# Padded loads of decays, keys and receptances, and an opening with five plain slices, in a recurrence with a gated MLP behind it

## The chip, the cores and the metric

The program runs on one core of one Trainium2 chip. The metric is device time in microseconds, from an execution without the profiler. The kernel before was executed three times for it: 574.48, 574.70 and 574.89 us, a median of 574.7 us. All durations below come from one further execution that the hardware profiler recorded.

## The reference

Four sequences, 8 heads of 48 channels and 768 steps go through a recurrence with a decay per channel; its output is the input of a gated MLP with 3072 rows, model width 384 and inner width 1536.

```python
for t in range(S):                       # r, k, v, w: [4, 8, 768, 48]
    cur = einsum('bhd,bhe->bhde', u[None] * kt, vt)
    y[:, :, t] = einsum('bhd,bhde->bhe', rt, state + cur)
    state = wt[:, :, :, None] * state + einsum('bhd,bhe->bhde', kt, vt)
x = y.transpose(0, 2, 1, 3).reshape(B * S, H * D)
gate = 1 / (1 + exp(-(x @ w_gate)))
out = (gate * (x @ w_val)) @ w_out
```

## The kernel before, in words

**Tiling.** The 768 steps are cut into six chunks of 128. A *unit* q is one chunk of one sequence; there are 24, and four units with consecutive q (one per sequence, the same chunk) make a round of 512 rows. For each unit the kernel loads two tiles. `pin` holds decays, keys and receptances with channels on 112 partitions, 1544 numbers in a row; `tok` holds receptances, keys and values with time on 128 partitions, 1152 numbers in a row. The attention of a unit is: running products of the decays on VectorE (`prep_k`, `prep_r`), a transposition of the keys (`turn_k`, tile `pk`), scores and sums on TensorE (`section1`, tile `pa`), a mask and the new state on VectorE (`mask`, `keep`), the output products (`section2`, tile `py`), a copy by ScalarE (`take_y`), a transposition (`turn_x`, tile `px`), and a copy that makes the MLP's input (`take_x`). GpSimd prepares the diagonal (`bonus1`, `bonus2`, `bonus4`, tiles `bon` and `at`).

**The MLP.** The inner width is cut into 12 slices f of 128. The weights of a slice come as words of 64 bits (`raw`) that VectorE turns into numbers of 32 bits in three steps (`w_body`, `w_sign`, `w_tail`), while ScalarE checks their range with two passes (`w_guard`, tile `sq`). A slice is then used in one of two ways. A *plain* slice is multiplied as float32 (lines 527 and 569). A *split* slice first gets a high and a low part (`w_hi`, `w_lo`), and so does x, and three products of float32r stand for one (lines 530, 533 and 573). For each slice there are a gate product (`pg`), a value product (`pu`), a sigmoid, VectorE's product of the two, and an output product (`po`). There is one bank for `pg` and one for `pu`.

**The order.** The rounds 1 to 5 have an order written out by hand, the same in every round. Round 0, the preparation of the weights, and the first units of round 1 together are the *opening*. Its order comes from a planner (class `Plan`) at build time: each operation has an engine, a cost, a rank and conditions, and a list scheduler emits the operations in the order in which its own clock starts them. `TURNS` gives the ranks, `COMES` the order in which loads are issued on SyncE's queue, `LATE` and `LAGS` shift ranks, `ROOM` counts buffers. On the chip each engine then runs its instructions strictly in that order, waiting where data is not there.

Before the change the slices 0 to 3 are plain in round 0, each in two groups of units, (0, 1) and (2, 3), 256 columns at a time; the slices 4 to 11 are split, with all 512 columns. Behind the scores of units 0 and 1 stand 11 and 12 products of the identity with itself (`busy`, line 451), whose result nothing reads.

Of the kernel before, what the change touches and what calls it, by code (L numbers as in the profile page):

```python
# [205 lines left out]
def tile_kernel(ctx: ExitStack, tc: tile.TileContext, dec: bass.AP, tok: bass.AP, wts: bass.AP, u: bass.AP, out: bass.AP):  # L206
# [86 lines left out]
    def place(q):  # L293
        return q % B * NC_ + q // B

    def load_pin(q):
        t = p2.tile([L, WW + 2 * NP * C], F32, tag="pin", name=f"pin{q}")
        if q == 0:
            nc.sync.dma_start(t[:, :WW], dec[place(q)][:, :WW])
            nc.sync.dma_start(t[:, WW:], dec[place(q)][:, WW:])  # L300
        else:
            nc.sync.dma_start(t, dec[place(q)])
        pin[q] = t
# [526 lines left out]
```

## Time and profile before

| | us |
|---|---|
| median of three runs | 574.7 |
| the profiled execution, its own time | 575.17 |
| its span from first to last instruction | 573.1 |
| TensorE busy | 548.7 (96%) |
| VectorE busy | 325.0 (57%) |
| ScalarE busy | 204.3 (36%) |
| GpSimd busy | 104.2 (18%) |
| start of the first MLP product (round 0) | 31.41 |
| start of the first MLP product of round 1 | 139.29 |

The profiled execution lies 0.47 us above the median, and 2.1 us of it lie outside the span. A row of the timeline gives the start and length of a run of like instructions on one engine, then line, operation, output and inputs, and in brackets how long the engine was idle before it and what ended that. TensorE's float32 instructions appear twice for each product in the program, so x6 stands for three products. Successive products overlap, so the pace of a run is read from the distance between starts, not from the length of one. VectorE and ScalarE instructions overlap by about 0.1 us in the same way.

### The profile page before, as it was taken

How to read it: one execution, taken by the hardware profiler on the slowest of the kernel's cores; microseconds unless marked ns; L12 is line 12 of the kernel's file. 1: busy time of each engine (PE TensorE's matmuls, PEld its weight loads, DVE VectorE, ACT ScalarE, POOL GpSimd, SP SyncE). 2: the span in 40 equal slices, each digit the busy share in tenths (PEclk: the TensorE clock that was granted, in tenths of full speed). 3: DMA queues.
4: the chain of work that ended last, by engine and by line, in shares of the span. 5: the costliest groups of instructions: out<-in, count | busy, mean ns of one | idle time of the engine just before them, and what ended most of it. 6: DMA issues, size and time to landing. Idle time of an engine off the chain costs nothing.

```text
span 573.1 us, 13259 instructions
## 1 busy us (share of the span) xinstructions
PE 548.7 (96%) x5910; PEld 452.3 (79%) x5910; DVE 325.0 (57%) x451; ACT 204.3 (36%) x376; POOL 104.2 (18%) x89
## 2 busy tenths in 40 slices
PE   5789999999999999999999999999999999999994
PEld 4667877888778888888888888878888888888883
DVE  4899999997774564653563653653643621321221
ACT  2565775734442322422223323222413322312111
POOL 4440634104022111221210220210220200000000
PEclk9799999999999999999999999999999999999999
DMA  8856927424213023123033133032122000100001
GB/s 251 267 173 249 312 78 270 117 66 147 73 46 91 21 72 91 63 85 91 1 92 91 56 91 91 2 91 92 55 92 65 27 2 2 55 2 0 1 0 61
DMA packets 11044, 50.57 MB, mean 88 GB/s; under 512 B 1265, under 2 KB 1266, under 8 KB 9442
## 3 DMA queue, kind: packets, MB, share of 16 engines
q1 hardware_dynamic: 8818, 45.70, 25.7%
q10 hardware_dynamic: 2160, 3.93, 1.8%
q8 instruction: 48, 0.79, 0.6%
q14 instruction: 18, 0.15, 0.1%
HBM read 44.91 MB, written 4.72 MB: 87 GB/s over the span
## 4 chain that ended last, share of the span: by engine, by line
PE 83%; DVE 9%; issue 2%; ACT 2%; DMA 1%; POOL 1%; SPq 0%; ACTq 0%; DVEq 0%; POOLq 0%
PE po L573 23%; PE pg L530 16%; PE pu L530 15%; PE pu L533 8%; PE pg L533 8%; PE py L432 3%; PE py L419 3%; PE pa L403 1%; PE pa L390 1%; PE pk L371 1%; DMA tok<-tok 1%; DVE temp L273 1%; PE px L486 1%; DVE raw L276 1%; PE busy L451 1%
## 5 line engine op out<-in xcount | busy, mean ns | idle before, releaser
L550 DVE TENSOR_TENSOR sg<-pu,sg 128x512 f32<-128x512 f32 (+1 forms) x76 | 50.3, 662 | 160.9 <-PE pu L533 155.8
L573 PE MATMUL po<-hh,w 128*128 128x512 f32 x408 | 129.6, 399 | 0.0
L530 PE MATMUL pg<-x,w 128*128 128x512 f32 x408 | 106.7, 397 | 0.0
L530 PE MATMUL pu<-x,w 128*128 128x512 f32 x408 | 104.3, 391 | 0.0
L530 PEld LDWEIGHTS pu<-x,w 128*128 128x128 f32 x408 | 76.3, 188 | 15.9
L530 PEld LDWEIGHTS pg<-x,w 128*128 128x128 f32 x408 | 75.0, 188 | 16.5
L573 PEld LDWEIGHTS po<-hh,w 128*128 128x128 f32 x408 | 74.2, 188 | 13.8
L543 ACT ACTIVATE sg<-pg 128x512 f32<-128x512 f32 (+1 forms) x76 | 43.4, 571 | 113.3 <-PE pg L533 109.7
L554 ACT CAST hh<-sg 128x512 fp32r<-128x512 f32 x68 | 42.2, 620 | 116.5 <-DVE sg L550 116.4
L573 PE MATMUL po<-hl,w 128*128 128x512 f32 x204 | 79.8, 391 | 0.1
L558 DVE TENSOR_TENSOR hl<-sg,hh 128x512 fp32r<-128x512 f32 x68 | 51.9, 763 | 42.3 <-ACT hh L554 42.2
L320 POOL TENSOR_TENSOR bon<-tok,ub 128x384 f32<-128x384 f32 x24 | 29.2, 1215 | 230.5 <-DMA tok<-tok 199.2
L533 PE MATMUL pg<-x,w 128*128 128x512 f32 x204 | 57.6, 391 | 0.0
L533 PE MATMUL pu<-x,w 128*128 128x512 f32 x204 | 57.6, 391 | 0.0
L333 POOL TENSOR_TENSOR at<-eye,a 128x512 f32<-128x512 f32 x24 | 32.4, 1351 | 119.2 <-DVE a L327 119.2
L573 PEld LDWEIGHTS po<-hl,w 128*128 128x128 f32 x204 | 38.4, 188 | 9.2 <-DVE hl L558 0.7
L533 PEld LDWEIGHTS pg<-x,w 128*128 128x128 f32 x204 | 38.3, 188 | 8.2
L533 PEld LDWEIGHTS pu<-x,w 128*128 128x128 f32 x204 | 38.3, 188 | 8.0
L323 POOL TENSOR_TENSOR bon<-bon,tok 128x384 f32<-128x384 f32 x24 | 39.6, 1650 | 1.9
L340 DVE TENSOR_TENSOR_SCAN eg<-pin,ends 112x516 f32<-112x516 f32 x24 | 35.9, 1495 | 7.0 <-DMA pin<-dec 7.0
L366 ACT ACTIVATE eg<-eg 112x1032 f32<-112x1032 f32 x24 | 25.6, 1068 | 36.6 <-DVE pin L362 35.4
L481 ACT COPY bon<-py 128x384 f32<-128x384 f32 x24 | 11.5, 478 | 61.3 <-PE py L432 61.3
(80 smaller groups left out, 654.2 us busy)
## 6 DMA issues: line engine op xcount, KB each, us to landing
pin<-dec SPq DMA_DIRECT2D x23, 675.5 KB, 6.2
tok<-tok SPq DMA_DIRECT2D x24, 576.0 KB, 6.1
raw<-wts SPq DMA_DIRECT2D x12, 1152.0 KB, 12.2
y<-o ACTq DMA_DIRECT2D x15, 256.0 KB, 2.0
y<-o SPq DMA_DIRECT2D x3, 256.0 KB, 3.4
pin<-dec SPq DMA_DIRECT2D x1, 448.0 KB, 4.8
pin<-dec SPq DMA_DIRECT2D x1, 227.5 KB, 3.6
line<-u SPq DMA_DIRECT2D x1, 1.5 KB
```

Source lines behind the costliest of these rows:

```text
L320: nc.gpsimd.tensor_tensor(out=bon[q], in0=tk[q][:, 0:DM], in1=ub, op=ALU.mult)
L323: nc.gpsimd.tensor_tensor(out=bon[q], in0=bon[q], in1=tk[q][:, DM:2 * DM], op=ALU.mult)
L333: nc.gpsimd.tensor_tensor(out=att[q], in0=eye.unsqueeze(1).unsqueeze(1).broadcast_to(shape), in1=a0, op=ALU.mult)
L340: nc.vector.tensor_tensor_scan(out=e[:, 516:0:-1], data0=t[:, 516:0:-1], data1=ends[:, 516:0:-1], initial=0.0, op0=ALU.mult, op1=ALU.add,)
L366: nc.scalar.activation(both, both, AF.Square, accum_out=acc_d[:, q:q + 1])
L530: nc.tensor.matmul(t, lhsT=w[f][:, cols], rhs=x[n][:, a, k, spot], start=k == 0 and j == 0, stop=False)
L533: nc.tensor.matmul(t, lhsT=whi[f][:, cols], rhs=x[n][:, 1, k, i0 * C:i1 * C], start=False, stop=k == NKT - 1)
L543: nc.scalar.activation(sg, hid["g", n, f, i0], AF.Sigmoid)
L550: nc.vector.tensor_tensor(out=sg, in0=hid["u", n, f, i0], in1=sg, op=ALU.mult)
L554: nc.scalar.copy(hh, hid["s", n, f, i0])
L558: nc.vector.tensor_tensor(out=hl, in0=hid["s", n, f, i0], in1=hid["hi", n, f, i0].bitcast(F32), op=ALU.subtract)
L573: nc.tensor.matmul(to, lhsT=w[f][:, cols], rhs=h, start=first and i == 0, stop=last and i == 2, skip_group_check=True)
```

## The change

**Loads.** The array `dec` on the host gets 128 rows of 1664 numbers for each unit instead of 112 rows of 1544. The keys begin at number 528 instead of 520. A load of `pin` moves 128 rows of 1552 numbers (unit 0 in two parts, 528 and 1024), and the rows 112 to 127 are not used.

**The opening.** Five slices are plain, 0 to 4, and seven are split. The plain slices 0, 1 and 4 are cut into three groups, unit 0 alone, unit 1 alone and units 2 and 3, so that 128 columns are multiplied at a time for the first two; 2 and 3 keep two groups. The planner's ranks and several of its costs are new. The products of the identity are 40 members of the planner's list with the lowest rank, instead of two runs at fixed places; they and the spreading of u use the banks of `po` until the MLP needs these.

```diff
-TURNS = "c0 w0 w1 c1 w2 c2 w3 c3 c4 c5 w4 w5 w6 w7 w8 w9 w10 c6 w11 c7"
-COMES = "p0 ub t0 p1 t1 w0 w1 w2 p2 t2 t3 p3 w3 p4 w4 t4 w5 w6 t5 p5 w7 t6 w8 t7 w9 w10 w11 p6 p7 p8 t8 t9 p9"
-GROUPS = [(0, 2), (2, 4)]
-WIDE = [4, 5, 6, 7, 8, 9, 10, 11]
-EXACT = [0, 1, 2, 3]
+TURNS = "c0 w0 w1 c1 w2 c2 w3 c3 c4 w4 w5 c5 w6 w7 w8 w9 w10 w11 c6 c7"
+COMES = "p0 ub w0 t0 w1 p1 w2 w3 t1 w4 t2 p2 t3 w5 p3 w6 t4 t5 p4 p5 t6 w7 w8 w9 w10 w11 p6 p7 t7 t8 p8 p9 t9"
+SINGLE = [0, 1, 4]
+WIDE = [5, 6, 7, 8, 9, 10, 11]
+EXACT = [0, 1, 2, 3, 4]
...
-        t = p2.tile([L, WW + 2 * NP * C], F32, tag="pin", name=f"pin{q}")
...
+        t = p2.tile([P, KW + 2 * NP * C], F32, tag="pin", name=f"pin{q}")
+        for i, j in ((0, KW), (KW, KW + 2 * NP * C)) if q == 0 else ((0, KW + 2 * NP * C),):
+            nc.sync.dma_start(t[:, i:j], dec[place(q)][:, i:j])
+        pin[q] = t[:L]
...
-        if q in BUSY:
-            t = ps1.tile([P, 512], F32, tag="po0", name=f"busy{q}")
-            for _ in range(BUSY[q]):
-                nc.tensor.matmul(t[:, :P], lhsT=ident, rhs=ident, start=True, stop=True)
...
+    def keep_busy():
+        nc.tensor.matmul(lull[:, :P], lhsT=ident, rhs=ident, start=True, stop=True)
+
+    lull = ps1.tile([P, 512], F32, tag="po0", name="lull")
+    for i in range(BUSY):
+        add(f"busy{i}", "PE", 0.43 if i < 9 else 0.28, [i and f"busy{i - 1}"], 1000 + i, keep_busy)
...
+    parts = {f: ([(0, 1), (1, 2), (2, B)] if f in SINGLE else [(0, 2), (2, B)]) if f in EXACT else [(0, B)] for f in range(NFF)}
...
-    dec = np.zeros((NG, L, WW + 2 * NP * C), np.float32)
+    dec = np.zeros((NG, P, ROW), np.float32)
```

**What moves, on SyncE's queue.** The first loads that SyncE issues before the change; `pin` and `tok` belong to the units 0, 0, 1, 1, 2 and 2 in turn, `raw` to the slices 0, 1 and 2:

```order
L299 DMA pin_106<-dec 112x520
L300 DMA pin_106<-dec 112x1024
L611 DMA line<-u 1x384
L307 DMA tok_110<-tok 128x1152
L302 DMA pin_118<-dec 112x1544
L307 DMA tok_130<-tok 128x1152
L258 DMA raw_181<-wts 128x1152
L258 DMA raw_248<-wts 128x1152
L258 DMA raw_314<-wts 128x1152
L302 DMA pin_368<-dec 112x1544
L307 DMA tok_381<-tok 128x1152
```

The same place in the changed kernel, with `raw` of the slices 0 to 4 and `tok` of the units 0, 1 and 2:

```order
L301 DMA pin_107<-dec 128x528
L301 DMA pin_107<-dec 128x1024
L603 DMA line<-u 1x384
L260 DMA raw_116<-wts 128x1152
L306 DMA tok_129<-tok 128x1152
L260 DMA raw_141<-wts 128x1152
L301 DMA pin_191<-dec 128x1552
L260 DMA raw_205<-wts 128x1152
L260 DMA raw_228<-wts 128x1152
L306 DMA tok_287<-tok 128x1152
L260 DMA raw_293<-wts 128x1152
L306 DMA tok_342<-tok 128x1152
```

The weights of slice 0 now stand ahead of `tok` of unit 0, and four slices ahead of `tok` of unit 1.

**On TensorE.** The first MLP products before the change, with what stands just ahead of them (`py` and `px` are of unit 1; `pg_0_0` is slice 0 of the group that begins with unit 0):

```order
L451 MATMUL busy_291<-ident 128x128 x12
L419 MATMUL py_327<-mid_318,pin_118 64x48 x8
L432 MATMUL py_327<-tok_130,at_306 32x48 x32
L486 MATMUL px_374<-ident,bon_193 128x128 x3
L527 MATMUL pg_0_0_387<-whole,raw_181 128x256 x3
L527 MATMUL pu_0_0_392<-whole,raw_181 128x256 x3
L527 MATMUL pg_0_1_405<-whole,raw_248 128x256 x3
L371 MATMUL pk_415<-ident,pin_368 128x112 x4
L569 MATMUL po_0_423<-sg_0_0_402,raw_181 128x256
L569 MATMUL po_1_424<-sg_0_0_402,raw_181 128x256
```

And in the changed kernel, from the first MLP product on:

```order
L519 MATMUL pg_0_0_349<-whole,raw_116 128x128 x3
L519 MATMUL pu_0_0_356<-whole,raw_116 128x128 x3
L519 MATMUL pg_0_1_367<-whole,raw_141 128x128 x3
L561 MATMUL po_0_374<-sg_0_0_360,raw_116 128x128
L561 MATMUL po_1_375<-sg_0_0_360,raw_116 128x128
L561 MATMUL po_2_376<-sg_0_0_360,raw_116 128x128
L519 MATMUL pu_0_1_383<-whole,raw_141 128x128 x3
L561 MATMUL po_0_374<-sg_0_1_388,raw_141 128x128
L561 MATMUL po_1_375<-sg_0_1_388,raw_141 128x128
L561 MATMUL po_2_376<-sg_0_1_388,raw_141 128x128
L418 MATMUL py_404<-mid_347,pin_191 64x48 x8
L431 MATMUL py_404<-tok_287,at_381 32x48 x32
```

The slices 0 and 1 of unit 0 are now multiplied ahead of the output products of unit 1 (`py_404`), which stood ahead of the first MLP product before.

**On ScalarE.** Around the first sigmoid before the change (`sq` are the range checks of slices 1 and 2):

```order
L265 ACTIVATE sq_322,acc_s<-raw_248 128x1152
L266 ACTIVATE sq_322,acc_t<-sq_322 128x1152
L481 COPY bon_193<-py_327 128x2x4x48
L514 CAST x_372<-whole 128x3x128
L509 ACTIVATE whole,acc_x<-px_374 128x3x128
L265 ACTIVATE sq_384,acc_s<-raw_314 128x1152
L266 ACTIVATE sq_384,acc_t<-sq_384 128x1152
L543 ACT_TABLE_LOAD
L543 ACTIVATE sg_0_0_402<-pg_0_0_387 128x256
L514 CAST x_372<-whole 128x3x128
L543 ACTIVATE sg_0_1_420<-pg_0_1_405 128x256
```

And in the changed kernel (`sq` of slices 3 and 4; `whole` is unit 0, `bon_305` is unit 1):

```order
L501 ACTIVATE whole,acc_x<-px_301 128x3x128
L467 COPY mid_347<-pa_307 112x192
L506 CAST x_353<-whole 128x3x128
L535 ACT_TABLE_LOAD
L535 ACTIVATE sg_0_0_360<-pg_0_0_349 128x128
L267 ACTIVATE sq_364,acc_s<-raw_228 128x1152
L268 ACTIVATE sq_364,acc_t<-sq_364 128x1152
L535 ACTIVATE sg_0_1_388<-pg_0_1_367 128x128
L267 ACTIVATE sq_390,acc_s<-raw_293 128x1152
L268 ACTIVATE sq_390,acc_t<-sq_390 128x1152
L476 COPY bon_305<-py_404 128x2x4x48
```

The range checks of slices 3 and 4 now stand between the first sigmoids and ahead of the copy of unit 1's output; three checks stood ahead of the first sigmoid before.

## Rows read from the trace of the kernel before

**Rows 1.** The page's first part: busy time of each engine, its share of the span and its instructions.

```profile
PE 548.7 (96%) x5910; PEld 452.3 (79%) x5910; DVE 325.0 (57%) x451; ACT 204.3 (36%) x376; POOL 104.2 (18%) x89
```

**Rows 2.** Busy time of each engine (TensorE's products and weight loads, VectorE, ScalarE, GpSimd) in a stretch of the span (in us), with the granted clock, the busy share of the 16 DMA engines and what they moved in GB/s.

```profile
200.00:300.00 100.00, 100.00 (x1053) 82.54 (x1052) 53.56 (x78) 29.39 (x58) 18.36 (x14) 1.00 0.24 72
```

**Rows 3.** TensorE's timeline in the opening.

```profile
5.07 1.61 PE L609 MATMUL spread<-line 1*128 1x384 f32 x2 [5.07 <-DMA line<-u]
...
8.72 1.13 PE L390 MATMUL pa<-pin 48*64 48x64 f32 x32 [0.46 <-DVE pin L362]
...
17.97 0.55 PE L486 MATMUL px<-ident,bon 128*128 128x128 f32 x3 [0.60 <-ACT bon L481]
...
21.98 0.88 PE L403 MATMUL pa<-tok,kT 64*64 64x48 f32 x23 [2.69 <-issue]
22.79 5.34 PE L451 MATMUL busy<-ident 128*128 128x128 f32 x24
28.06 0.67 PE L419 MATMUL py<-mid,pin 48*64 48x48 f32 x16
28.66 0.88 PE L432 MATMUL py<-tok,at 64*32 64x48 f32 x64
...
31.41 1.57 PE L527 MATMUL pg<-whole,raw 128*128 128x256 f32 x6 [0.67 <-ACT whole L509]
...
38.77 1.46 PE L527 MATMUL pu<-whole,raw 128*128 128x256 f32 x6
40.06 1.46 PE L527 MATMUL pg<-whole,raw 128*128 128x256 f32 x6
...
99.16 1.53 PE L530 MATMUL pg<-x,w 128*128 128x512 f32 x6
...
105.29 1.52 PE L530 MATMUL pg<-x,w 128*128 128x512 f32 x6
...
139.29 1.53 PE L530 MATMUL pg<-x,w 128*128 128x512 f32 x6
```

**Rows 4.** Whom TensorE waited for from its first MLP product to the first of round 1 (31.4 to 139.29 us): total in us, times, longest.

```profile
PE pg L527 <- ACT sg L543: 1.4, 1, 1.4
PE po L569 <- DVE sg L550: 0.9, 3, 0.4
PE pg L527 <- ACT whole L509: 0.7, 1, 0.7
PE pk L371 <- ACT whole L509: 0.7, 1, 0.7
PE py L419 <- DVE state L478: 0.5, 1, 0.5
```

**Rows 5.** The same columns as Rows 2, for three stretches chosen by what the queue carried in them: weights of slices 0 to 2; `pin` and `tok` of unit 2; `pin` of units 6 and 7 alone.

```profile
12.00:20.00 8.00, 6.33 (x146) 5.62 (x145) 7.90 (x11) 2.69 (x7) 6.51 (x4) 1.00 1.01 428
20.00:26.00 6.00, 4.02 (x38) 3.93 (x38) 4.46 (x6) 4.69 (x8) 0.26 (x1) 0.58 0.94 223
102.00:107.00 5.00, 5.00 (x24) 4.14 (x23) 4.96 (x6) 3.85 (x6) 0.55 (x1) 1.00 0.90 227
```

**Rows 6.** VectorE's timeline in the opening.

```profile
4.57 1.23 DVE L340 TENSOR_TENSOR_SCAN eg<-pin,ends 112x516 f32<-112x516 f32 x1 [4.57 <-DMA pin<-dec]
...
7.97 0.69 DVE L362 TENSOR_TENSOR pin<-pin,eg 112x512 f32<-112x512 f32 x1
11.69 0.55 DVE L327 TENSOR_REDUCE a<-bon 128x8 f32<-128x384 f32 x1 [3.02 <-POOL bon L323]
...
14.78 0.72 DVE L463 COPY_PREDICATED at<-after,pa 128x512 f32<-128x512 int32 x1
15.41 0.34 DVE L478 TENSOR_TENSOR state<-pa,mid 112x192 f32<-112x192 f32 x1
...
16.91 1.31 DVE L362 TENSOR_TENSOR pin<-pin,eg 112x512 f32<-112x512 f32 x1
...
18.61 0.75 DVE L270 TENSOR_SCALAR temp<-raw 128x1152 int32<-128x1152 int32 x1
19.39 2.08 DVE L273 SCALAR_TENSOR_TENSOR temp<-raw,temp 128x1152 int32<-128x1152 int32 x1
...
23.60 1.34 DVE L276 SCALAR_TENSOR_TENSOR raw<-raw,temp 128x1152 int32<-128x1152 int32 x1
```

**Rows 7.** ScalarE's timeline: the guard of the running products, the copy that makes x of unit 0, the two passes of a range check, and the loading of the sigmoid's table.

```profile
18.32 1.07 ACT L366 ACTIVATE eg<-eg 112x1032 f32<-112x1032 f32 x1 [0.40 <-DVE pin L362]
...
19.38 0.47 ACT L509 ACTIVATE whole<-px 128x384 f32<-128x384 f32 x1
...
19.85 1.27 ACT L265 ACTIVATE sq<-raw 128x1152 bf16<-128x1152 f32 x1
...
21.24 1.16 ACT L266 ACTIVATE sq<-sq 128x1152 bf16<-128x1152 bf16 x1
...
33.93 1.28 ACT L543 ACT_TABLE_LOAD   x1
```

**Rows 8.** TensorE's timeline in two stretches inside the first run of identity products.

```profile
11.40 2.77 PE L451 MATMUL busy<-ident 128*128 128x128 f32 x12
...
13.96 1.06 PE L451 MATMUL busy<-ident 128*128 128x128 f32 x7
```

**Rows 9.** The columns of Rows 2 for the stretch around the second run of identity products.

```profile
21.10:27.80 6.70, 5.82 (x46) 5.73 (x46) 5.12 (x7) 4.20 (x9) 0.51 (x1) 0.50 0.68 159
```

More of the change, by code (lines that the diff above doesn't have):

```diff
@@ L29 @@
 WW = 520
+KW = 528
+ROW = 13 * P
 NFF = DFF // P
@@ L493, in plain @@
     def plain(q):
-        return q < (B if EXACT else 2)
-    def shared(q):
-        return plain(q) and len(WIDE if q < 2 else EXACT) < (NFF if q >= 2 else NFF + 1) and (q >= 2 or WIDE)
+        return q < B
     def take_x(q):
@@ L502, in take_x @@
             if q == 0:
-                whole[0] = p2.tile([P, NKT, (B if EXACT else 2) * C], F32, tag="x", name="whole")
+                whole[0] = p2.tile([P, NKT, B * C], F32, tag="x", name="whole")
             to = whole[0]
@@ L629, in tile_kernel @@
         add(f"pr{q}", "DVE", 1.93, [f"pk{q}"], k + 0.1, prep_r, q)
-        add(f"guard{q}", "ACT", 1.26, [f"pr{q}", old and f"fade{q}"], k + 0.5, guard, q, give=["eg"])
+        add(f"guard{q}", "ACT", 1.26, [f"pr{q}", old and f"fade{q}"], k + LATE["gd"], guard, q, give=["eg"])
         if q == ahead:
@@ L634, in tile_kernel @@
         add(f"kT{q}", "ACT", 0.53, [f"tk{q}"], k + 0.1, take_k, q, give=["bank"])
-        add(f"s1_{q}", "PE", 1.3, [f"kT{q}", f"tok{q}", f"pr{q}"], k + 0.15, section1, q, take=["pair"], give=["kT"])
+        add(f"s1_{q}", "PE", 1.05, [f"kT{q}", f"tok{q}", f"pr{q}"], k + 0.15, section1, q, take=["pair"], give=["kT"])
         add(f"mid{q}", "DVE" if old else "ACT", 0.36, [f"s1_{q}", old and f"fade{q}"], k + 0.1, middle, q, take=["mid"])
@@ L638, in tile_kernel @@
         add(f"keep{q}", "DVE", 0.36, [f"mid{q}"], k + 0.15, keep, q)
[L639 removed]
+        add(f"s2_{q}", "PE", 1.25 if q < B else 1.45, [f"mk{q}", f"keep{q}"], k + 0.2, section2, q, give=["at", "pin", "mid"] + ["ready"] * old)
         add(f"y{q}", "ACT", 0.5, [f"s2_{q}"], k - 1, take_y, q, give=["pair"])
[L641 to L642 removed]
+        add(f"tx{q}", "PE", 0.36, [f"y{q}", q % B and f"tx{q - 1}"], k + 0.4, turn_x, q, take=["bank"] + ["x"] * (q in (0, B)), give=["bon"])
+        add(f"xh{q}", "ACT", 0.68, [f"tx{q}"], k, take_x, q, give=["bank"] * plain(q))
         if plain(q):
[L644 to L646 removed]
+            add(f"xp{q}", "ACT", 0.54, [f"xh{q}", q and f"xp{q - 1}"], k + LATE["xl"], part_x, q, take=["x"] * (q == 0))
+            add(f"xl{q}", "DVE", 0.5, [f"xp{q}"], k + LATE["xl"], rest_x, q)
         else:
@@ L659, in tile_kernel @@
             past = SPLITS[i - 1]
-            used = [f"wl{past}", f"wg{past}"] + [f"dn{g}_{past}" for g in range(2) if past not in WIDE and (not g or past in EXACT)] if i else []
+            used = [f"wl{past}", f"wg{past}"] if i else []
             add(f"wh{f}", "ACT", 1.15, [f"wt{f}"] + used, k + LATE["wl"], w_hi, f)
             add(f"wl{f}", "DVE", 1.36, [f"wh{f}"], k + LATE["wl"], w_lo, f)
-    tall = [f for f in range(NFF) if f not in WIDE]
-    for g, (i0, i1) in enumerate(GROUPS + [(0, B)]):
-        m, some = i1 - i0, tall if g < 2 else WIDE
-        for f in some:
-            e = g == 0 or g == 1 and f in EXACT
-            a, name = (0, f, i0, i1, e), f"{g}_{f}"
-            k = 100 + f + LAGS[g]
+    parts = {f: ([(0, 1), (1, 2), (2, B)] if f in SINGLE else [(0, 2), (2, B)]) if f in EXACT else [(0, B)] for f in range(NFF)}
+    past = {}
+    for f in range(NFF):
+        e = f in EXACT
+        for i0, i1 in parts[f]:
+            m = i1 - i0
+            a, name = (0, f, i0, i1, e), f"{i0}_{f}"
+            k = 100 + f + LAGS[i0 if e else 3]
             soon = k / 1000 - 1
-            past = some[some.index(f) - 1] if f != some[0] else None
             up_cost = 12 * (0.002 + 0.0533 * m) if e else 9 * (0.0135 + 0.0533 * m)
+            before = [past[i] for i in range(i0, i1) if i in past]
             need = [f"xh{i}" if e else f"xl{i}" for i in range(i0, i1)] + [f"wt{f}" if e else f"wl{f}"]
-            need += [past is not None and f"pu{g}_{past}", g == 1 and f"pu0_{f}"]
-            add("pg" + name, "PE", up_cost, need, k, gate, *a, take=["pg", "unit"])
+            add("pg" + name, "PE", up_cost, need + ["pu" + p for p in before], k, gate, *a, take=["pg", "unit"])
             add("sg" + name, "ACT", 0.14 + 0.13 * m, ["pg" + name], soon, sigmoid, *a, give=["pg"])
```

73 lines of the change are left out of this document (32 added, 41 removed).

## The prediction, made before the changed kernel was run

> **What bounds the kernel now.** I read the page's busy shares first. TensorE is busy for 548.7 us, 96% of the span [rows 1], so a gain must come from time in which TensorE stands idle or does what nothing reads. The stretches of the span say where that is not: from 200 to 300 us TensorE is busy for 100.00 of 100 us [rows 2]. TensorE's timeline of the opening shows the rest [rows 3]. The first product of the MLP starts at 31.41 us. Ahead of it stand the attention of units 0 and 1, and between its parts waits and identity products: one run of 24 passes lasts 5.34 us. From 31.41 us to the first product of round 1 at 139.29 us TensorE waits for 4.2 us in all [rows 4]. So the start of round 1 sets the end, and it equals the start of the first MLP product, plus work, plus waits. The change adds nothing but one pair of splitting passes (high and low part of slice 4) to round 1, where VectorE has half of its time free [rows 2]. I forecast the shift of round 1's start and carry it to the end.
>
> **The loads.** Weights alone move at 428 GB/s with all DMA engines busy; the `pin` loads of units 6 and 7 alone move at 227, with the engines busy for 0.90 of the time, and `pin` and `tok` of unit 2 together at 223 [rows 5]. The bytes are not what costs: a load of `pin` is 112 x 6176 B = 0.69 MB, 3.0 us at 227 GB/s. With 128 rows of 6208 B it is 0.79 MB, which takes 1.9 us at the weights' rate and 3.5 us at the old one. I take 1.9, because the new load has the weights' shape (128 rows), and keep 3.5 for a rival. `tok` (0.59 MB) then takes 1.4 us and a slice of weights (1.18 MB) 2.8 us.
>
> [...]
>
> **The way to the first MLP product.** VectorE could start at 4.57 us [rows 6], when the first part of `pin` landed. I take 3.8 us for it (3.5 to 4.6 as bounds), and behind it on the queue, at 0.42 MB per us: slice 0 at 7.8, `tok` of unit 0 at 9.2, slice 1 at 12.0, `pin` of unit 1 at 13.9, slice 2 at 16.7, slice 3 at 19.5, `tok` of unit 1 at 20.9.
> - VectorE's preparation of unit 0 takes 4.1 us (4.57 to 8.66) [rows 6] and ends at 7.9; the first two steps on slice 0 (0.75 and 1.35, or 2.08 in one row) end at 10.0. Then it must wait for the new state, which needs ScalarE's copy of the sums of unit 0.
> - TensorE now runs 8 identity products, the spreading of u, 4 more, the transposition, 5 more, and only then the scores. With the clock granted at 0.50 a pass costs 0.22 us (24 in 5.34) [rows 3, 9]. The first run before has this pace in its middle (12 in 2.77) and at most 0.15 at its end (7 in 1.06) [rows 8], so TensorE got faster within that run. A product is two passes. The spreading starts at about 5.07 with the landing of u and takes 1.61 [rows 3]; the nine products behind it take 2.7 us at 0.15 and 4.0 at 0.22, the transposition 0.6 to 1.0, scores and sums 1.1 to 1.9 (the scores alone took 1.13 [rows 3]). I take the faster pace, as eight products come first: scores and sums end at 10.9, at the slower pace at 13.5.
> - ScalarE's range check of slice 0 (1.27 + 1.16 us and two readouts [rows 7], 2.6 together) stands ahead of the copy of the sums and ends at 10.5. The copy ends at 11.2, the state at 11.6.
> - VectorE: third step on slice 0 (1.34) to 12.9, the reduction (0.55) to 13.4, first step on slice 1 to 14.1, keys of unit 1 (from 12.2 to 14.8 in the rows of before, 2.6) to 16.7, the mask (0.72) to 17.4 [rows 6].
> - Output products of unit 0 1.5 us (28.06 to 29.6 for unit 1) to 18.9, copy and transposition 1.1 to 20.0 [rows 3].
> - ScalarE: the guard of unit 1 stands ahead of the copy that makes x. It needs the receptances of unit 1, which VectorE has at about 21.2 (one more weight step, 1.34, then the 2.5 that it took from 15.7 to 18.2 [rows 6]). Guard 1.26 and copy 0.66 [rows 7] end at 23.1.
>
> So the first MLP product starts at 23.1 us instead of 31.41: **-8.3 us**, with 21.5 and 27 as bounds. Idle time of VectorE (3.02 us ahead of 11.69 [rows 6]) and the second run of identity products (5.34 us [rows 3]) pay for it; all 40 products now lie in front of that point.
>
> **What is given back.**
> - Output products and transposition of unit 1 stood ahead of 31.41 us and now come after the first MLP product: 1.5 + 0.4 = **+1.9 us**.
> - The fifth plain slice: three products of 256 columns take 1.29 us (38.77 to 40.06), so a plain slice costs 6 x 1.29 = 7.7; a split slice costs 6.13 (99.16 to 105.29) [rows 3]. **+1.6 us** for TensorE. VectorE saves a low part of the weights and one of the hidden tile and pays a few small products; I count nothing, since TensorE bounds that stretch.
> - Pieces of 128 columns: six passes at half of 0.216 us would be free; at 0.15 [rows 8] they cost 0.25 more than half of 1.29. There are nine pairs, so 0 to 4.5 us; the 0.15 holds slow passes and the full length of the last, so I stay near the low end: **+0.5 us**.
> - Waits. The table of the sigmoid (1.28 us [rows 7]) stands behind two copies, so the second gate starts at 25.5 with the one bank: 1.0 us. The check of slice 3 (2.6) stands ahead of the second sigmoid: 1.2 us. The check of slice 4 stands ahead of the copy of unit 1's output: 0.6, and x of unit 1 then costs the 0.7 of before. That is 3.5; the later waits of before, 4.2 - 1.4 - 0.7 = 2.1 [rows 4], I keep. 5.6 against 4.2: **+1.4 us**.
>
> Sum: -8.3 + 1.9 + 1.6 + 0.5 + 1.4 = -2.9 us. The profiled execution took 575.2 us, so 572.3; it lies 0.5 above the median of the runs, so I predict **571.8 us** for the runs.
>
> **Rivals.**
> 1. *More is gained.* First MLP product at 21.5 us, pieces free, waits no more than before: -9.9 + 1.9 + 1.6 = -6.4, 568.3 us. For it: VectorE begins on the weights some 10 us earlier than before (18.61 [rows 6]). Against it: every step above hands over between engines.
> 2. *The padding brings nothing.* `pin` at 3.5 us instead of 1.9, twice ahead of the first gate: +3.2, 575.0 us. For it: why the rows are slow is not in the trace; against it: the shape argument above.
> 3. *The clock falls.* From 21.1 to 27.8 us the clock was granted at 0.50 [rows 9], the lower level, after TensorE had been idle for 2.69 us [rows 3]; it cost little, as mostly identity products ran. In the new order MLP products run there. My steps hold idle times of one to two us on TensorE near 16 and 20 us. Half a clock for 6.7 us costs up to 3.3: 575.1 us. [...]
> 4. *Slower: ScalarE's range checks hold the gates.* There is one gate bank, and round 0 has 20 gates instead of 16; the checks of slices 3 to 6 (2.6 us each) stand among the first of them. If each holds TensorE for all of its length, the waits are 10.4 us where I counted 2.8, and the sum is +4.7: 579.4 us. It decides from the point where these waits exceed my count by 2.9 us; half of the excess gives 575.6. Against it: three checks and the table stood ahead of the first sigmoid before, and TensorE waited 1.4 us for sigmoids in all [rows 4].
>
> **How the numbers follow.** Chances: forecast 0.62 (own range 569 to 574.3), rival 1 0.10, rival 2 0.08, rival 3 0.07, rival 4 0.13. About 0.2%, 1.15 us, is what a measurement of this kernel can tell from no change, so faster means below 573.5 and slower above 575.9. Faster: nearly all of the forecast and rival 1, 0.70. Same: the rest of the forecast, rivals 2 and 3, 0.17. Slower: rival 4, 0.13. The range goes from 567.0, beyond rival 1, to 576.2, which leaves out the far half of rival 4.
>
> **What would show it.** Stretches in which `pin` alone moves should stand above 400 GB/s (rival 2: near 227). The first MLP product should start between 21.5 and 27 us, with the clock at 1.00 from there on (rival 3: a stretch at 0.50). TensorE's waits from there to round 1 should sum to 4 to 8 us, with the sigmoid and the copy of unit 1's output as the largest (rival 4: over 9, all on ScalarE). The first product of round 1 should start near 136.4 us, and from there to the end the two traces should agree within 1 us. If round 1 starts as predicted and the end does not follow, the forecast is wrong in taking the rest as unchanged.

## The result, and the profile after

The changed kernel takes **580.08 us** (median of four runs, 579.67 to 580.86); the kernel before 574.80 (four, 574.48 to 575.86). The ratio is 1.0091, with a 95% interval of 1.0074 to 1.0109: slower by 5.3 us, where 571.8 was predicted. The profiled execution took 579.67 us, its span is 577.9.

| | before | predicted | after |
|---|---|---|---|
| first MLP product, us | 31.41 | 23.1 | 24.75 |
| first product of round 1 | 139.29 | 136.4 | 141.56 |
| between the two | 107.88 | 113.3 | 116.81 |
| from there to the start of the last MLP product | 426.08 | 426.1 | 428.99 |

So the opening won 6.7 us, round 0 lost 8.9, and the rounds 1 to 5, which the prediction took as unchanged, lost 2.9. The page's first part answers to [rows 1], the stretch from 200 to 300 us to [rows 2]:

```profile
PE 556.9 (96%) x6007; PEld 460.2 (80%) x6007; DVE 320.6 (55%) x454; ACT 205.4 (36%) x379; POOL 101.8 (18%) x89
```

```profile
200.00:300.00 100.00, 99.98 (x1175) 82.41 (x1168) 51.63 (x78) 28.83 (x57) 19.85 (x14) 1.00 0.22 79
```

TensorE is busy all the time there, as before, and the clock was granted in full. A look at busy shares finds nothing; what changed is the pace of a pass, which the timeline shows. Here are a gate, a value and the start of an output product of the last round, without attention between them, first of the kernel before, then of the kernel after:

```profile
551.29 1.52 PE L530 MATMUL pg<-x,w 128*128 128x512 f32 x6
...
553.33 1.52 PE L530 MATMUL pu<-x,w 128*128 128x512 f32 x6
...
555.37 0.61 PE L573 MATMUL po<-hh,w 128*128 128x512 f32 x2
```

```profile
500.41 1.54 PE L522 MATMUL pg<-x,w 128*128 128x512 f32 x6
...
502.47 1.54 PE L522 MATMUL pu<-x,w 128*128 128x512 f32 x6
...
504.53 0.62 PE L565 MATMUL po<-hh,w 128*128 128x512 f32 x2
```

From start to start nine passes take 2.04 us before and 2.06 after, 226.7 and 228.9 ns for one: 1% on every pass of this stretch.

TensorE's timeline of the new opening, which answers to [rows 3, 8]:

```profile
1.44 3.78 PE L605 MATMUL lull<-ident 128*128 128x128 f32 x16 [1.44 <-POOL ident masks.py:199]
...
9.34 2.37 PE L605 MATMUL lull<-ident 128*128 128x128 f32 x10
11.64 1.13 PE L389 MATMUL pa<-pin 48*64 48x64 f32 x32
12.54 0.77 PE L402 MATMUL pa<-tok,kT 64*64 64x48 f32 x32
13.24 4.51 PE L605 MATMUL lull<-ident 128*128 128x128 f32 x38
19.39 0.58 PE L370 MATMUL pk<-ident,pin 112*128 112x112 f32 x4 [1.64 <-issue]
...
24.75 0.97 PE L519 MATMUL pg<-whole,raw 128*128 128x128 f32 x6 [0.43 <-ACT whole L501]
25.56 0.87 PE L519 MATMUL pu<-whole,raw 128*128 128x128 f32 x6
```

Identity passes take 0.23 us until about 12 us (10 from 9.34 to 11.64). The views read a granted clock of 1.00 there too, but the first clock record of this trace begins at 12.87 us (14.18 in the kernel before), so the trace shows no grant for these passes. And whom TensorE waited for from 24.7 to 141.6 us (total, times, longest), which answers to [rows 4]:

```profile
PE po L561 <- DVE sg L542: 1.5, 4, 0.5
PE px L481 <- ACT bon L476: 1.3, 2, 0.7
PE py L418 <- DVE state L473: 1.1, 2, 0.7
PE py L431 <- issue: 0.9, 1, 0.9
PE pg L519 <- issue: 0.7, 1, 0.7
PE pk L370 <- ACT whole L501: 0.7, 1, 0.7
PE py L418 <- DVE at L458: 0.6, 1, 0.6
PE pg L519 <- ACT sg L535: 0.5, 1, 0.5
PE pg L519 <- ACT whole L501: 0.4, 1, 0.4
```

The loads did what was hoped. The last two of these stretches, in which only `pin` moved, answer to the last line of [rows 5] (units 4 and 5; 6 and 7): 422 GB/s instead of 227. The first line is from the start of the program, where the queue was slower.

```profile
4.00:8.00 4.00, 4.00 (x14) 2.70 (x14) 3.53 (x5) 0.48 (x1) 0.00 (x0) 1.00 0.89 290
...
60.40:61.90 1.50, 1.50 (x12) 1.42 (x11) 0.93 (x3) 1.21 (x1) 1.42 (x2) 1.00 1.04 422
...
94.00:95.40 1.40, 1.40 (x8) 1.15 (x7) 1.40 (x3) 1.40 (x4) 0.43 (x1) 1.00 1.01 422
```

I took TensorE's time between the first gate and round 1 apart, each product from its start to the next start, breaks over 0.15 us set aside:

| us | before | after | difference | predicted |
|---|---|---|---|---|
| plain slices (4, then 5) | 32.66 | 43.42 | +10.76 | |
| split slices (8, then 7) | 51.81 | 44.38 | -7.43 | |
| both together | 84.47 | 87.80 | +3.33 | +2.1 |
| attention | 19.74 | 21.57 | +1.83 | +1.9 |
| breaks | 3.67 | 7.43 | +3.76 | +1.4 |

By what ended them, the waits of [rows 4] and of the list above are 2.8 and 2.9 us for ScalarE, 1.4 and 3.4 for VectorE, and 0.2 and 1.6 called issue (waits of 0.2 us that stand below the lists are counted in). So the new waits are not ScalarE's.

### The profile page after: what moved, and what is told of

The parts are those of the page before. It is cut to its first block, busy times and chain, and to the rows that moved or that the text cites. A ratio compares the mean times of both kernels' runs of the same rounds, so it can differ in the third digit from the quotient of the medians.

```text
span 577.9 us, 13471 instructions
## 1 busy us (share of the span) xinstructions
PE 556.9 (96%) x6007; PEld 460.2 (80%) x6007; DVE 320.6 (55%) x454; ACT 205.4 (36%) x379; POOL 101.8 (18%) x89
## 4 chain that ended last, share of the span: by engine, by line
PE 86%; DMA 4%; DVE 3%; POOL 2%; issue 2%; SPq 1%; ACT 1%; ACTq 0%; POOLq 0%; DVEq 0%
PE po L565 24%; PE pg L522 16%; PE pu L522 16%; PE pu L525 8%; PE pg L525 8%; DMA tok<-tok 4%; PE py L431 3%; PE py L418 3%; PE pa L389 1%; PE po L561 1%; PE pa L402 1%; PE pk L370 1%; PE pu L519 1%; PE px L481 1%; PE pg L519 1%
## 5 line engine op out<-in xcount | busy, mean ns | idle before, releaser
L542 DVE TENSOR_TENSOR sg<-pu,sg 128x512 f32<-128x512 f32 (+2 forms) x80 | 51.0, 637 | 170.1 <-PE pu L525 163.3
L565 PE MATMUL po<-hh,w 128*128 128x512 f32 x402 | 127.7, 399 | 0.0
L522 PE MATMUL pg<-x,w 128*128 128x512 f32 x402 | 105.5, 397 | 0.4 <-issue 0.4
L522 PE MATMUL pu<-x,w 128*128 128x512 f32 x402 | 103.1, 392 | 0.0
L522 PEld LDWEIGHTS pu<-x,w 128*128 128x128 f32 x402 | 75.3, 188 | 16.4
L522 PEld LDWEIGHTS pg<-x,w 128*128 128x128 f32 x402 | 73.9, 188 | 16.8 <-issue 0.6
L535 ACT ACTIVATE sg<-pg 128x512 f32<-128x512 f32 (+2 forms) x80 | 44.1, 551 | 116.2 <-PE pg L525 106.6
L319 POOL TENSOR_TENSOR bon<-tok,ub 128x384 f32<-128x384 f32 x24 | 32.2, 1341 | 211.2 <-DMA tok<-tok 104.6
L525 PE MATMUL pu<-x,w 128*128 128x512 f32 x201 | 57.0, 392 | 0.0
L525 PE MATMUL pg<-x,w 128*128 128x512 f32 x201 | 56.9, 391 | 0.0
L332 POOL TENSOR_TENSOR at<-eye,a 128x512 f32<-128x512 f32 x24 | 28.9, 1206 | 145.2 <-DVE a L326 145.2
L525 PEld LDWEIGHTS pu<-x,w 128*128 128x128 f32 x201 | 37.8, 188 | 8.3
L525 PEld LDWEIGHTS pg<-x,w 128*128 128x128 f32 x201 | 37.7, 188 | 8.3 <-DVE x L511 0.2
L322 POOL TENSOR_TENSOR bon<-bon,tok 128x384 f32<-128x384 f32 x24 | 37.7, 1572 | 1.9
```

Source lines behind the costliest of these rows:

```text
L319: nc.gpsimd.tensor_tensor(out=bon[q], in0=tk[q][:, 0:DM], in1=ub, op=ALU.mult)
L322: nc.gpsimd.tensor_tensor(out=bon[q], in0=bon[q], in1=tk[q][:, DM:2 * DM], op=ALU.mult)
L332: nc.gpsimd.tensor_tensor(out=att[q], in0=eye.unsqueeze(1).unsqueeze(1).broadcast_to(shape), in1=a0, op=ALU.mult)
L522: nc.tensor.matmul(t, lhsT=w[f][:, cols], rhs=x[n][:, a, k, spot], start=k == 0 and j == 0, stop=False)
L525: nc.tensor.matmul(t, lhsT=whi[f][:, cols], rhs=x[n][:, 1, k, i0 * C:i1 * C], start=False, stop=k == NKT - 1)
L535: nc.scalar.activation(sg, hid["g", n, f, i0], AF.Sigmoid)
```

## The experiments

Sixteen further programs ran. Ratios are to the kernel before on the same chip; its medians lay between 574.8 and 575.6 us.

| | us | ratio (95%) |
|---|---|---|
| e1_after_x_back | 578.35 | 1.0049 (1.0031 to 1.0068) |
| e2_before_x_off | 577.31 | 1.0038 (1.0020 to 1.0056) |
| e3_before_padded | 573.53 | 0.9963 (0.9951 to 0.9975) |
| e4_after_tok1_early | 583.32 | 1.0126 (1.0087 to 1.0166) |
| e5_no_pieces | 581.38 | 1.0120 (1.0079 to 1.0162) |
| e6_four_plain | 582.73 | 1.0141 (1.0104 to 1.0177) |
| e7_no_fillers | 576.31 | 1.0017 (1.0000 to 1.0035) |
| e8_before_x_128 | 582.06 | 1.0117 (1.0069 to 1.0165) |
| e9_padded_no_fillers | 574.44 | 0.9988 (0.9971 to 1.0006) |
| e10_thin_fillers | 582.46 | 1.0124 (1.0091 to 1.0157) |
| e12_before_x_256 | 575.44 | 1.0007 (0.9985 to 1.0029) |
| e13_before_hh_off | 577.10 | 1.0030 (1.0014 to 1.0047) |
| e14_combined | 570.55 | 0.9931 (0.9905 to 0.9957) |
| e15_after_shifted | 575.97 | 1.0017 (0.9996 to 1.0039) |
| e16_padded_shifted | 571.12 | 0.9942 (0.9916 to 0.9969) |
| e17_padded_again | 573.02 | 0.9977 (0.9961 to 0.9993) |

### Where the operands lie

The addresses that the built programs give their tiles differ in one thing that reaches the rounds: `pin` has two buffers, each 32 B wider per partition, so that all that lies behind them (x, `hh`, `hl`) begins 64 B behind a multiple of 256 B instead of at one. An unused tile (`margin`) ahead of them can move them back, or move those of the kernel before. The first diff is to the changed kernel.

```diff
-        p1.tile([P, 72], F32, name="margin")
+        p1.tile([P, 56], F32, name="margin")
```

> The changed kernel with one number altered: the unused tile ahead of the second pool has 56 instead of 72 numbers per partition, so that x, hh and hl begin again at multiples of 256 B, as in the kernel before, instead of 64 B behind one (the two wider pin buffers had moved them). Theory A (the 64 B cost each pass of TensorE some 2 ns): the six passes of a gate product go from 1373 to 1360 ns, the nine of an output product from 2060 to 2040, and the time falls by about 0.96% of the 540 us of such passes, 5 us, to 575 us. Rival B (the pace comes from the chip, the profile or the length of the code): 1373 ns stays and the time is 580 within 1 us. The opening and the waits of round 0 stay in both.

The opposite edit in the kernel before (72 to 88):

> The kernel before with the same unused tile at 88 instead of 72 numbers: x, hh and hl begin 64 B behind a multiple of 256, nothing else is altered. Theory A: 1360 ns becomes 1373 ns, 2040 becomes 2060, and the time rises by about 5 us to 580. Rival B: 574.7 within 1 us and 1360 ns.

The pace followed the address in both. The same three products in e1, then value and output product in e2:

```profile
502.38 1.52 PE L522 MATMUL pg<-x,w 128*128 128x512 f32 x6
...
504.42 1.52 PE L522 MATMUL pu<-x,w 128*128 128x512 f32 x6
...
506.46 0.61 PE L565 MATMUL po<-hh,w 128*128 128x512 f32 x2
```

```profile
501.26 1.54 PE L530 MATMUL pu<-x,w 128*128 128x512 f32 x6
...
503.32 0.62 PE L573 MATMUL po<-hh,w 128*128 128x512 f32 x2
```

2.04 us in e1, 2.06 in e2: theory A is shown. Its size was not 5 us, though. (The profile of e1 is that of its slowest execution, 581.24 us where the median is 578.35, with a lower granted clock in round 0: 0.88 from 32 to 36 us, 0.70 from 36 to 40. Its rounds 1 to 5 can be compared, its round 0 hardly.) In e2 the rounds 1 to 5 take 428.41 us against 426.08, **2.3 us** more. The last round, which has no attention, bears the full 1% (76.35 against 75.65), the other four 0.2 to 0.8 each: where attention is mixed in, an output product takes 2148 ns in e2 instead of 2162 in the kernel before (medians of rounds 2 to 5), a little less.

What counts within 256 B was tried with 128 and 256 B, and with the second set of tiles alone (a further unused tile of 8 numbers in the second pool):

> The kernel before with x, hh and hl 128 B behind a multiple of 256 B (unused tile of 104 numbers; e2_before_x_off had 64 B). If what counts is 128 B, six passes take 1360 ns as in the kernel before and the time is that of before, 575.5; if it is 256 B, 1373 ns and 577.3 us as with 64 B.

> The kernel before with x, hh and hl moved by 256 B (unused tile of 136 numbers), so that they are at multiples of 256 B again. If the place within 256 B is what counts: 1360, 680 and 2040 ns as in the kernel before, 575.3 us. If the distance that they were moved counts (64 B cost 2.1 ns per pass, 128 B some 5): 1410 ns or more for six passes and over 585 us.

> The kernel before with only the second set of tiles (sg, hh, hl and the output tile) 64 B behind a multiple of 256 B, x at a multiple. If the start of the tile that streams through TensorE counts: the gate's six passes, which stream x, stay at 1360 ns, the output product's nine, which stream hh and hl, go from 2040 to 2060, and the time rises by a third of what e2_before_x_off cost (1.8 us), 0.5 to 0.9 us. If it is the place of something else, both stay or both change.

| start of x behind a multiple of 256 B | six passes, ns | three | nine |
|---|---|---|---|
| 0 (before, e1, e12 after 256 B) | 1360 | 680 | 2040 |
| 64 (after, e2) | 1373 | 687 | 2060 |
| 128 (e8) | 1396 | 695 | 2090 |
| 0, but hh and hl at 64 (e13) | gate 1389, value 1364 | gate 697, value 680 | output 2077 |

Columns are medians in the last round. e12 shows that the place within 256 B counts and not the distance. e8 fits neither of its two forecasts, since 128 B cost more than 64. e13 was half wrong: the output products slow down, by more than forecast (2077 ns for 2060), but the gates do too (1389 ns for 1360), although by the program's addresses x has not moved, and the values, which stream the same x, hardly do. It costs 2 us instead of 0.5 to 0.9. What lies behind the slower pace is open.

### The padding alone

> The kernel before with the padded loads alone (128 rows of 6208 B, keys from column 528), x, hh and hl kept at multiples of 256 B. If the padding is worth what the prediction took (a load of pin in 1.9 us instead of 3.0), pin alone moves at over 400 GB/s, pin of unit 1 lands 2 to 3 us earlier, and as the opening of the kernel before waits for VectorE too, the first MLP product comes 0 to 2.5 us earlier than 31.41: 572.5 to 574.7 us. If the padding brings nothing: 227 GB/s, more bytes, 574.7 to 576 us.

It is the padded load and the host's array in the kernel before, with `margin` at 56. From 8 to 12 us, with `pin` and `tok` of the first units on the queue, 232 GB/s moved in the kernel before; here it is the weights' rate (the kernel before, then e3):

```profile
8.00:12.00 4.00, 3.54 (x72) 3.19 (x71) 0.98 (x2) 1.91 (x4) 2.00 (x2) 1.00 1.02 232
```

```profile
8.00:12.00 4.00, 4.00 (x75) 3.73 (x74) 1.42 (x2) 1.90 (x4) 2.79 (x3) 1.00 1.03 423
```

The first gate comes at 29.80 instead of 31.41, and round 1 at 137.54 instead of 139.29. The padding is worth 0.1 to 0.5% by itself (e3, and e17, which is e3 once more), and rival 2 is out. The edit gives the load 128 rows and rows that start at multiples of 256 B; no run tells which of the two counts.

### The list: loads, pieces, slices

All three start from e1. `COMES` with tok of unit 1 earlier, no pieces, and four plain slices:

```diff
-COMES = "p0 ub w0 t0 w1 p1 w2 w3 t1 w4 t2 p2 t3 w5 p3 w6 t4 t5 p4 p5 t6 w7 w8 w9 w10 w11 p6 p7 t7 t8 p8 p9 t9"
+COMES = "p0 ub w0 t0 w1 p1 t1 w2 w3 w4 t2 p2 t3 w5 p3 w6 t4 t5 p4 p5 t6 w7 w8 w9 w10 w11 p6 p7 t7 t8 p8 p9 t9"
```

> The changed kernel with x, hh and hl back at multiples of 256 B and tok of unit 1 loaded right after pin of unit 1, ahead of slices 2 and 3 (in the changed kernel behind them, landing at 22.68 us). Theory C (round 0 loses time because unit 1 comes late): tok of unit 1 lands near 17 us, the mask of unit 1 moves from 31 to some 27 us, and the waits of TensorE between the first gate and round 1 fall from 7.4 us to 5 or 6; the time is 1 to 2.5 us under that of e1_after_x_back. Rival D (the lateness of unit 1 is covered by the products on unit 0 alone): no difference over 0.5 us, or a loss, as slices 2 and 3 come 1.4 us later.

The tile landed at 18.29 instead of 22.66 us and the mask of unit 1 ran at 28.44 instead of 30.91, as theory C has it. But the planner laid out a new list around it; TensorE waited in the opening (busy for 1.79 of 4 us from 16 to 20), its clock was granted at 0.57 from 20 to 24 us and at 0.50 from 24 to 28, the first gate came at 28.25, round 1 at 146.37. A late tok is not shown as a cause, nor excluded.

```diff
-SINGLE = [0, 1, 4]
+SINGLE = []
```

> As e1_after_x_back, without pieces of 128 columns: slices 0, 1 and 4 take units 0 and 1 together. Theory P (the pieces cost TensorE some 2.6 us, five plain slices at 8.68 us against 8.17 in the kernel before, but the work on unit 0 alone fills 5 us that would else be idle): the first gate moves from 24.7 us to about 35.5 us, the plain slices fall to about 8.2 us each, and round 1 starts 1 to 3 us later than in e1; 579 to 581 us. Rival Q (what TensorE does ahead of unit 1 only has to be waited for elsewhere, on VectorE, so the early start is worth nothing): round 1 starts 2 to 3 us earlier than in e1; 575 to 576.5 us.

581.4 us; first gate 36.89, round 1 147.32, 3 us later than in e1's profile: theory P and not rival Q. The plain slices fell to 42.06 / 5 = 8.41 us, a part of them at the lower clock (0.50 from 28 to 40 us). As the clock and the planner's list changed with the edit, the run does not give the price of the pieces alone.

```diff
-SINGLE = [0, 1, 4]
-WIDE = [5, 6, 7, 8, 9, 10, 11]
-EXACT = [0, 1, 2, 3, 4]
+SINGLE = [0, 1]
+WIDE = [4, 5, 6, 7, 8, 9, 10, 11]
+EXACT = [0, 1, 2, 3]
```

> As e1_after_x_back, with four plain slices instead of five (slice 4 split, its pieces gone). By the trace a plain slice takes 8.68 us of TensorE and a split one 6.34, so 2.3 us go. If TensorE bounds round 0, the time falls by 2 to 2.5 us, to about 576; if VectorE bounds it (it has to make high and low parts of slice 4 inside round 0, some 2.5 us more), the waits of TensorE grow by as much and the time stays within 0.7 us of e1, 578.3.

582.7, worse than both forecasts. New waits on VectorE's low parts appear in round 0 (1.2 us for a hidden tile, 0.7 for weights), which speaks for VectorE; but waits of another kind, the next topic, are mixed in (3.3 us in all, against 3.0 in e1), and the run does not settle it.

### The identity products, and a wait without a cause

> As e1_after_x_back with one identity product instead of 40 and the same order of all else. Theory F (the identity products hold the clock up): the granted clock falls to 0.50 in stretches between 8 and 30 us, the first gate comes 1 to 4 us later than 24.7 and the first MLP products run at half pace for a while: 579 to 582 us. Rival G (the work ahead of the first gate is bound by other engines, and the clock does not matter there): first gate at 24.7 us or earlier, time within 0.7 us of e1, 578.3, or below.

**Faster** than e1, 1.0017 against 1.0049. The half of theory F on the pace holds: without the products TensorE is slow until 28 us (the first gate's row has 1.65 us where the changed kernel's has 0.97) and the gate comes at 26.82. The granted clock, which theory F wanted at 0.50, reads 1.00 in all stretches, but the views read 1.00 also where a trace has no clock record, so that half stays open. Everything behind the first gate is better, and from 150 us to the end the list of TensorE's waits is empty. In e1 it has this row there, in the kernel after one of 1.1 us and one of 0.4, in the kernel before one of 1.0:

```profile
PE py L431 <- issue: 1.8, 2, 1.4
```

"issue" says that the profile shows no releaser. I counted TensorE's instructions (weight load and product of each pass, and one for each semaphore instruction) and looked up where these waits stand. In the kernels before, after, e1, e3, e5, e6 and e9 there are 18 waits over 0.15 us that stand at position 193 or 194 of a block of 256 instructions (17 called issue, and one of e5 that the profile puts down to ScalarE), among them the 2.69 us at 21.98 of [rows 3]. Nine others called issue stand elsewhere, so it is the position that tells these waits, and not the word. The trace has the other half: each ends 2.2 to 2.7 us after the start of a packet of 16 KB on the DMA queue that the page calls "instruction" (q8; 2.24 to 2.58 us in the kernels before and after). The kernel after has 49 such packets for some 12,070 instructions of TensorE, one for 246, and counted in blocks of 256 the waits fall on one position. So I take such a packet for the fetch of a block of 256 instructions; that is an estimate from these counts. In the kernel after such a packet starts at 310.06 us, and TensorE goes on at 312.48, in the middle of the products of unit 15 (the queue's line of the stretch 310.0 to 311.1, and the row of the timeline):

```profile
q8 instruction: 1, 0.02, 5.5%
```

```profile
312.48 0.23 PE L431 MATMUL py<-tok,at 64*32 64x48 f32 x2 [1.07 <-issue]
```

A unit's attention in the rounds is a run of some 320 instructions for passes of 13.9 ns from start to start (kernels before and after); it uses up a block in 1.8 to 1.9 us (e7, from the border at 372.1 us to the next at 374.0). Over fourteen kernels a border that stood up to 292 instructions into such a run cost nothing, but for one (0.7 us at 263, in e6); at 298 it cost 0.0 to 0.3 us, at 300 to 318 it cost 1.0 to 1.8, all 14 times. There the whole block before it lay inside the run too, and the fetch, which began 0.6 to 0.8 us after the border before (1.4 in e13), was not back, as I read it.

Two tries did not tell code from work. e9 takes the identity products out of e3, e10 makes each of them one column wide in e1:

> As e3_before_padded (list, slices and order of the kernel before, padded loads, x, hh and hl at multiples of 256 B), without the 23 identity products. Theory K (a code block of 16 KB that TensorE fetches too late holds it: every wait of TensorE called issue so far ended 2.2 to 2.7 us, where much else was moving 3.4, behind the start of such a fetch; where the block borders fall depends on the number of instructions ahead): the waits of 2.3 us at 20.4 and of 1.4 us at 373.4 of e3 go or move, the first gate comes 1 to 4 us earlier than 29.8, and the time is 570 to 572.5 us. Theory F (the products hold the clock up): the clock falls, the first gate comes later, 573.5 to 576 us.

> As e1_after_x_back, each identity product with 1 column instead of 128: as many instructions as e1, next to no busy time. Theory K: the waits behind code fetches stand where they stand in e1 (sum about 5 us, against none over 0.4 us in e7_no_fillers) and the time is that of e1, 577.5 to 579. Rival W (what costs in e1 is the work of the identity products, or the clock that falls behind them): the waits are gone as in e7 and the time is 575.5 to 577.

In e9 the wait at 373 us went, and two others came at positions 193 and 194, 1.5 us at 242 and 1.3 at 266; the first gate's products ran at half pace (2.93 us in the gate's row for 1.57 in e3), and 574.4 us is what theory F gave, although the gate came earlier than in e3 (28.85 for 29.80). In e10 the waits stand at the same instructions as in the kernel after (1.2, 1.0 and 1.4 us), as theory K says, but TensorE kept the half pace until 31 us (1.65 us in the first gate's row), its first gate came at 29.1, and the time is that of neither theory.

So the code was moved and next to nothing else: tiny products ahead of everything (20 in e1, 80 instructions, which took 2.3 us of TensorE; 4 in e3, 16 instructions). The diff is to e1.

```diff
     lull = ps1.tile([P, 512], F32, tag="po0", name="lull")
+    for _ in range(20):
+        nc.tensor.matmul(lull[:32, :32], lhsT=ident[:32, :32], rhs=ident[:32, :32], start=True, stop=True)
```

> As e1_after_x_back, with 20 identity products of 32 by 32 put ahead of everything, 80 instructions of TensorE that take some 1 us while it has nothing to do. Theory K (only the place of the block borders counts): the border that stood 298 and 313 instructions into the runs of units 14 and 15 goes to 218 and 233; the waits of 0.3 and 1.4 us there vanish and no other run gets one, the rounds take 425 to 426 us instead of 427.5, the wait of 1.25 us at the first product of slice 2 goes too, the first gate stays within 0.5 us of 24.7, and the time is 575.5 to 577 us. Rival W (the identity products' own work or the clock behind them is what costs): waits and time of e1, 578.3 within 0.7.

> As e3_before_padded, with 4 identity products of 32 by 32 ahead of everything: 16 instructions. Theory K: the border in the run of unit 18 goes from 300 to 284 instructions in, the wait of 1.4 us at 373 us vanishes and none comes; the time is 1.0 to 1.6 us under e17_padded_again, 572 to 572.5. Rival W: same as e17 within 0.4 us.

> e3_before_padded once more, on the chip of e14 to e16: 573.5 us, the wait at the run of unit 18 again between 1.0 and 1.8 us.

TensorE's waits from 150 us on in e17, then in e16, then in e15:

```profile
PE py L431 <- issue: 1.2, 1, 1.2
PE pk L370 <- issue: 1.0, 1, 1.0
```

```profile
PE pk L370 <- PE pu L532: 0.7, 1, 0.7
```

```profile
PE pk L370 <- PE pu L525: 0.7, 1, 0.7
```

The waits on `py` left both kernels, at the two places computed ahead. (The second row of e17 stands at no border, at position 204; e15 and e16 wait 0.7 us there too.) e16 is 1.9 us under e17 (571.12 and 573.02, one chip), more than the 1.0 to 1.6 forecast. In the profiles the rounds are 1.65 us shorter, 1.2 of it by this wait, and the first gate is 1.1 us earlier, as the wait at position 193 ahead of it fell from 2.6 to 1.65 us; the part behind the last product is 1.3 us longer. e15 has a ratio of 1.0017 where e1 had 1.0049, with the same work and the first gate at 25.24, a little outside the forecast. Its round 0 got two waits that the forecast had not, 0.8 us at 27.04 and 0.4 at 85.05, both at position 193. That the place of the borders makes these waits is shown; rival W is out for them.

> As e3_before_padded, with 8 full identity products ahead of everything (TensorE gets to the full pace earlier, and the code moves by 32 instructions) and 8 instead of 12 in the second run of them, so that the rounds' code is 16 instructions later, as in e16. Theory K and theory F together: no wait at 373 us, the second run of identity products ends 1 to 2 us earlier and no longer holds the output products of unit 1, first gate at 27 to 28.5 us instead of 29.8, time 570.5 to 572 us. If the clock falls behind the shorter second run, the first MLP products run at half pace and the time is 573 to 574.

570.55 us, the lowest median, 0.7% under the kernel before, though not clear of e16's 571.12. Its opening:

```profile
1.44 3.50 PE L612 MATMUL lull<-ident 128*128 128x128 f32 x16 [1.44 <-POOL ident masks.py:199]
...
18.21 2.05 PE L450 MATMUL busy<-ident 128*128 128x128 f32 x16
23.17 0.67 PE L418 MATMUL py<-mid,pin 48*64 48x48 f32 x16 [2.91 <-DVE state L477]
...
26.88 2.93 PE L526 MATMUL pg<-whole,raw 128*128 128x256 f32 x6 [0.67 <-ACT whole L508]
```

The second run of identity products now ends at 20.3 us instead of 26.1 in e17, and no longer holds unit 1. The shorter run has the price that was feared: behind 2.9 us of idleness the first gate runs at half pace (2.93 us in its row against 1.57 in e16).

## Why the prediction was wrong

**The loads: right in their rate, 1.8 us late.** 422 GB/s against the 428 that I took. The landings are 1.8 us late from slice 0 on (9.59 for 7.8, tok of unit 1 at 22.68 for 20.9), one delay at the start carried along: from 4 to 8 us the queue moved 290 GB/s, where the prediction took 420. In e3, with the old list, the padding brought the rate as well (423 GB/s for 232 from 8 to 12 us); whether by the shape, on which the prediction built, or by the new start addresses is not shown.

**The way to the first gate: right, 1.65 us late.** 24.75 for 23.1, within its bounds. Scores and sums of unit 0 ended at 13.2 us, near the slow bound of 13.5 and not at 10.9, the new state came at 14.1 instead of 11.6, the keys of unit 1 at 19.3 instead of 16.7. TensorE's slow pace looks like the step that slipped, but e1 had the full pace from 5 us on, and its first gate came at 24.68. Two rows of its TensorE, identity products (8 passes in 1.00 us, from start to start) and the sums of unit 0:

```profile
5.68 1.16 PE L605 MATMUL lull<-ident 128*128 128x128 f32 x8
...
11.18 1.10 PE L402 MATMUL pa<-tok,kT 64*64 64x48 f32 x32 [2.19 <-ACT sq L267]
```

The sums begin with the landing of `tok` of unit 0 (11.04 us, where 9.2 was predicted). So does GpSimd (11.19), for which VectorE's reduction then waits 0.9 us; it begins at 15.20, hardly ahead of the changed kernel's 15.29. So the late loads hold the way even where TensorE is fast; that they account for all of the 1.65 us is likely and not shown. (The 1.64 us called issue at 19.39 is that wait: it ends at the same time in e15, 80 instructions further on, and e7 names VectorE's keys there.) Rival 3 stayed out of this profile, but with the same list the clock fell to 0.70 from 36 to 40 us in the profile of e1.

**Given back in round 0: short by 3.5 us, and the waits failed.** Unit 1's products +1.8 for +1.9. The fifth plain slice 32.66 / 4 - 51.81 / 8 = +1.7 for +1.6; that this fits is luck, as both prices were too low (8.17 for 7.7, 6.48 for 6.13). The pieces 43.42 - 5 x 32.66 / 4 = +2.6 for +0.5: the low end of 0 to 4.5 was the wrong choice, as a piece of six passes took 0.70 to 0.81 us where half of 1.29 is 0.65. The split slices came out 0.95 shorter than 7 x 51.81 / 8. The breaks +3.8 for +1.4, and not where they were forecast: the prediction added waits for ScalarE (gates, checks, copies) and counted nothing for VectorE, "since TensorE bounds that stretch". ScalarE's waits grew by 0.1 us and VectorE's by 2.0 (its product of gate and value 1.5 for 0.9, the new state 1.1 for 0.5, a mask 0.6 where there was none); 1.6 us are the two code fetches at 44.09 and 86.70, for which the prediction had no step.

**The rounds 1 to 5: this step failed.** "The change adds nothing but one pair of splitting passes" to them overlooked that wider `pin` buffers move every tile behind them. That costs 2.3 us (e2; between e1 and the changed kernel it is 1.45, or 1.7 without the code fetches); the rest of the 2.9, but for 0.1, is code fetches, 1.07 and 0.41 us against 0.99 in the kernel before. The 100.00 us of 100 of TensorE in [rows 2] (99.98 in the changed kernel) showed that nothing waits there, not that a pass keeps its length.

**Together.** 1.65 + 3.5 + 2.9 = 8.05 us over the forecast of 572.3; the tail behind the last product and what lies outside the span are 0.7 shorter, which leaves the 7.4 measured.

**The rivals.** Rival 4's 579.4 is close to the result by accident: ScalarE accounts for 1.3 + 0.7 + 0.5 + 0.4 = 2.9 us of TensorE's waits where it asked for over 9. With the tiles put back and the code moved (e15) the new list is within 0.4% of the kernel before. Against e16, which has the old list, the same loads and neither of the two costs, it is 4.9 us slower: it wins 3.1 us at the first gate and pays 7.9 up to round 1, 5.3 of it work (109.2 us of products against 103.9) and 2.6 waits. Starting the MLP earlier by cutting it into smaller and dearer pieces did not pay in this list as a whole; which part of the list costs what is open, since without the pieces (e5) and with four plain slices (e6) it was slower still.

## What to carry to other kernels

When a tile gets wider, print the start addresses of all tiles behind it, and compare the distance between starts of equal passes in the two traces before anything else; a busy share of 100% hid a pace that was 1% off here (226.7 and 228.9 ns a pass). When instructions are added or taken away on TensorE, even ones that cost nothing, work out where the block borders of its code fall in the runs of short passes; four tiny products ahead of all else were worth 1.9 us here, though 20 of them also brought two new waits in e15. And test a load's new shape and a new list apart: one brought about 2 us, the other cost 5, and the sum told of neither.

## What the runs showed of the hardware that I had not expected

- A pass of 512 columns took, in the last round, 226.7 ns with x, hh and hl at multiples of 256 B (before, e1), 228.9 with them 64 B behind (after, e2) and about 232 with 128 B (e8); 256 B further it was 226.7 again (e12).
- A packet of 16 KB on the queue q8 took 0.9 to 1.9 us (kernels before and after), and TensorE, in the 18 waits counted, went on 2.2 to 2.7 us after the start of one; in these programs such a wait can be told by its place, 193 or 194 instructions into a block of 256 of TensorE's.
- The views can read a granted clock of 1.00 while TensorE is at half pace: in e10 from 28 to 31 us, with six passes of a gate in a row of 1.65 us, against 0.97 in the kernel after. In the kernel after they read 1.00 ahead of the trace's first clock record at 12.87 us, about where its pace changed; whether e10's 1.00 is on record is not shown.
